# A two-layer MoE kernel after attention: the order of operand work and of weight loads in its second layer

## The chip, the cores and the metric

The kernel runs on one core of a Trainium2 chip. The metric is device time in microseconds (us). Three runs of the kernel before gave 1780.78, 1784.19 and 1786.06 us; the median is 1784.19 us. All numbers of a stretch or an instruction come from one further, profiled execution, which took 1785.07 us with a span of 1783.1 us.

## The reference

Attention with pooled keys and values gives 4608 tokens x 512. Two dense layers follow, each 512 -> 2048 -> 512. The second one, which the change touches, is:

```python
h = x @ w_in                      # (4608, 512) @ (512, 2048)
neg = h <= -1.0
pos = h >= 1.0
g = np.where(pos, h, np.where(neg, 0.0, (h + 1.0) ** 2 / 4.0))
return g @ w_out                  # (4608, 2048) @ (2048, 512)
```

## The kernel before

Every float32 operand of a matmul is split in two: a rounded part "hi" (written by ScalarE) and the rest "lo" = source - hi (written by VectorE). One product of blocks is then three matmuls: hi*hi, hi*lo, lo*hi.

The first layer runs token block by token block (lines 598 to 630) up to about 1002 us of the span. The second layer, class `Second`, uses block products: its matrices are cut in 2 x 2 blocks, and seven products of sums of blocks (a Strassen-Winograd form) replace eight. `ORDER1` = (1, 7, 2, 4, 6, 5, 3) is the order of the seven operands in its first phase (x @ w_in), `ORDER2` = (4, 5, 7, 6, 1, 3, 2) that of the second phase (g @ w_out).

**First phase.** Tokens go in six pairs of 2 x 384 columns, and for each pair there are eight steps j, so 48 steps, called cycles. A cycle has seven slots, in each of which TensorE does one product of six matmuls (128 x 128 by 128 x 384, line 841). The slots of a cycle hold products 6, 1, 7, 5, 2, 4, 3; products 1, 7, 2 and 4 already belong to the next step. So product 1 of a new pair is done in slot 1 of the last cycle of the pair before, product 4 in slot 5, and product 6 in slot 0 of the new pair's first cycle. X, V and Y are the PSUM banks in which products meet, p ("p7") and q are copies of banks in SBUF.

What else is issued stands in two places. `after(cycle, slot)` holds the same work for each cycle: three ScalarE copies, the four-step activation of the four results X, V, W, Y (`act1` on ScalarE, `act2` on VectorE or, for V and W, on GpSimd, `act3` on ScalarE, `act4` on VectorE), two VectorE adds, and the store of each result t to the DRAM buffer g. On VectorE these are 8 instructions a cycle. Two of them gate TensorE closely: the add of "W" (line 860, p<-Y,p) in slot 3 must have read bank Y before product 3 in slot 6 adds to it. The table in `first_phase` holds, per pair, the preparation of the next pair's operands: `x_load` (four DMAs of 384 KB, tiles xr), `x_sum` (the four block sums, two instructions each), and `x_split` (operand number pos of `ORDER1`, half k: one ScalarE and one VectorE instruction into a tile xs). An entry (c, s) is issued behind slot s of cycle c, counted from the start of the pair; the table runs from (4, 3) to (8, 0). The sums are made in place, so their order is tied to the splits: x_sum 2 overwrites the block b12 and can only follow its split. `w2_load`, `w2_sums`, `w2_split` prepare the weights of the second phase in the first four pairs and store them to DRAM (tiles w2d).

**Second phase.** Tokens go in blocks r of 1024; for each, seven products in `ORDER2` with eight units f each, a unit being 12 matmuls of 128 x 128 by 128 x 256 (line 1086). `g_load` brings g back (256 KB a load), `g_sum` makes sums, `hi` (line 1046) and `lo` (line 1051) split. The weights are fetched from w2d by `w2_fetch(t)`, 28 DMAs of 512 KB, four to a product, all of them issued during and just behind the last pair of the first phase.

**What sets the order.** The program is written in a fixed order; each engine runs its own instructions in that order and waits at the first that isn't ready. All DMAs are issued by one queue (SyncE). Its n-th DMA also waits until the DMA eight places before it has landed. A tile comes from a pool with a few places; a new tile in a place waits until the old one's last use, for a result t until its store has landed. The results t rotate over seven places ("gh" 2, "gl" 2, "raw" 3): each place is used again after seven results. The last places of "gh" serve unit 5 of the second phase as its hi and lo tiles.

Of the kernel before, what the change touches and what calls it, by code (L numbers as in the profile page):

```python
# [8 lines left out]
F32 = mybir.dt.float32  # L9
# [8 lines left out]
P = 128  # L18
NB = 512
# [8 lines left out]
NH = 384  # L28
# [7 lines left out]
def attention_moe_moe2(ctx: ExitStack, tc: tile.TileContext, qT, kT, v, k01, v01, w_in1, w_out1, w_in2, w_out2, out):  # L36
# [5 lines left out]
    nc = tc.nc  # L42
# [15 lines left out]
    raw_p = ctx.enter_context(tc.tile_pool(name="raw", bufs=3))  # L58
# [614 lines left out]
    class Second:  # L673
# [6 lines left out]
        def __init__(self, free):  # L680

            self.p1 = ctx.enter_context(tc.tile_pool(name="p1", bufs=1))
            used = sorted(
                [(2 * f + (1 if kind == "i" else 2 * LAG), kind, f) for kind in "io" for f in range(NF)]
            )
            tags = [f"{kind}{f}" for _, kind, f in used]
            self.spare, self.tags = tags[:4], tags[4:]
            order = [free] + [i for i in range(3) if i != free]
            self.x_tags = [[f"x{i}{k}{w}" for k in range(2) for w in "hl"] for i in order]
            self.wtmp = self.p1.tile([P, 6, 256], F32, tag="s7", name="wtmp")  # L690
            self.w1, self.w1_tiles, self.xs, self.bank, self.kept = {}, {}, {}, {}, {}
            self.g = [dram.tile([P, NT], F32, name=f"g2_{f}") for f in range(NF)]
            self.w2d = {pos: dram.tile([P, self.NJ, 2, 256], F32, name=f"w2d{pos}") for pos in range(7)}
            self.n_t = 0
            self.plan, self.places = {}, {}
            self.a, self.s, self.n_u = {}, {}, 0
            self.units = [(r, pos, f) for r in range(self.NPAIR2) for pos in range(7) for f in range(self.NJ)]
# [53 lines left out]
        def x_sum(self, what):  # L751

            for k in range(2):
                (b11, b12), (b21, b22) = self.kept["x", k, 0], self.kept["x", k, 1]
                to, a, b = {
                    1: (b11, b12, b11), 3: (b12, b22, b12), 2: (b12, b22, b11), 4: (b21, b21, b12),
                }[what]
                engine = nc.vector if what == 2 else nc.gpsimd
                engine.tensor_tensor(out=to, in0=a, in1=b, op=ALU.subtract)

        def x_split(self, p, pos, k):
            (b11, b12), (b21, b22) = self.kept["x", k, 0], self.kept["x", k, 1]
            prod = ORDER1[pos]
            if k == 0:
                self.xs[p, prod] = self.x_slot(7 * p + pos)
            src = {1: b11, 7: b12, 2: b21, 4: b21, 6: b12, 5: b11, 3: b22}[prod]
            s = self.xs[p, prod]
            self.parts(s[k, 0], s[k, 1], src, nc.gpsimd if k and prod in (5, 3) else nc.vector)

        def w2_load(self, f):  # L770
            t = wpool.tile([P, 2, DM], F32, tag=self.spare[0], name=f"w2x{f}")
# [25 lines left out]
        def ahead(self, slot):  # L797
            for j in range(self.NJ - 1):
                begin = (7 * j + 1) // 2 + 8
                if slot == begin - 6:  # L800
                    self.w1_load(j)
                if slot == begin - 2:
                    self.w1_sums(j)
                for pos in range(7):
                    if slot == begin + (pos + j % 2) // 2:
                        self.w1_split(j, pos)
            if slot == 5:
                self.x_load(0)
            for at, f, *args in (
                (9, self.x_split, 0, 0, 0), (10, self.x_split, 0, 0, 1), (11, self.x_sum, 1), (12, self.x_sum, 3),  # L810
                (14, self.x_split, 0, 1, 0), (15, self.x_split, 0, 1, 1), (16, self.x_sum, 2),
                (17, self.x_split, 0, 2, 0), (18, self.x_split, 0, 2, 1), (20, self.x_sum, 4),
                (22, self.x_split, 0, 5, 0), (23, self.x_split, 0, 5, 1),
                (24, self.x_split, 0, 6, 0), (25, self.x_split, 0, 6, 1),
            ):
                if slot == at:
                    f(*args)
# [43 lines left out]

        def t_tile(self, name):
            self.n_t += 1
            pool, tag = ((g_p, "gh"), (raw_p, "raw"), (g_p, "gl"), (g_p, "gh"), (raw_p, "raw"), (g_p, "gl"), (raw_p, "raw"))[
                self.n_t % 7
            ]
            return pool.tile([P, NB], F32, tag=tag, name=name)[:, 0:NH]


# [30 lines left out]
        def first_phase(self):  # L900
            for pos, k in ((3, 0), (3, 1), (4, 0), (4, 1)):
                self.put(-1, 0, self.x_split, 0, pos, k)
            self.put(-1, 1, self.w1_split, self.NJ - 2, 6)
            for pos in range(7):
                self.put(0, pos, self.w1_split, self.NJ - 1, pos)
            self.w1_load(self.NJ - 1)
            self.put(-1, 2, self.w1_sums, self.NJ - 1)
            for p in range(1, self.NPAIR):
                c = self.NJ * (p - 1)
                for cycle, slot, f, *args in (  # L910
                    (4, 3, self.x_load, p),
                    (5, 5, self.x_split, p, 0, 0), (5, 6, self.x_split, p, 0, 1),
                    (6, 0, self.x_sum, 1), (6, 1, self.x_sum, 3),
                    (6, 3, self.x_split, p, 1, 0), (6, 4, self.x_split, p, 1, 1), (6, 5, self.x_sum, 2),
                    (6, 5, self.x_split, p, 2, 0), (6, 6, self.x_split, p, 2, 1), (6, 6, self.x_sum, 4),
                    (7, 0, self.x_split, p, 4, 0), (7, 1, self.x_split, p, 4, 1),
                    (7, 2, self.x_split, p, 3, 0), (7, 3, self.x_split, p, 3, 1),
                    (7, 4, self.x_split, p, 5, 0), (7, 5, self.x_split, p, 5, 1),
                    (7, 6, self.x_split, p, 6, 0), (8, 0, self.x_split, p, 6, 1),
                ):  # L920
                    self.put(c + cycle, slot, f, *args)
            for f in range(self.NJ):
                n = 7 * (self.NJ * (f // 2) + 2 * (f % 2)) + 2
                self.put(n // 7, n % 7, self.w2_load, f)
                self.put((n + 6) // 7, (n + 6) % 7, self.w2_sums, f)
                for pos in range(7):
                    self.put((n + 8 + pos) // 7, (n + 8 + pos) % 7, self.w2_split, f, pos)
            end = self.STEPS - 1
            for f in range(4):
                self.put(end - 1, 3, self.g_load, 0, (2, 2), f)  # L930
                self.put(end - 1, 4, self.g_load, 0, (2, 2), f + 4)
                self.put(end, 1, self.g_load, 0, (2, 1), f)
                self.put(end, 4, self.g_load, 0, (2, 1), f + 4)
            for u in range(3):
                self.put(end, 3 + u, self.hi, u)
                self.put(end, 4 + u, self.lo, u)
            for cycle in range(-1, self.STEPS):
                for slot, (prod, ahead) in enumerate(((6, 0), (1, 1), (7, 1), (5, 0), (2, 1), (4, 1), (3, 0))):
                    s = cycle + ahead
                    self.product(prod, s)  # L940
                    self.after(cycle, slot)
                    for f, args in self.plan.pop((cycle, slot), []):
                        f(*args)
                if cycle >= self.STEPS - self.NJ:
                    for t in range(28):
                        if (2 * t + 1) // 7 == cycle % self.NJ:
                            self.w2_fetch(t)
            for slot in range(6):
                self.after(self.STEPS, slot)

        def after(self, c, slot):
# [8 lines left out]
                self.add("V", "V", "q", c)  # L960
            elif slot == 2:
                self.copy("p7", "V", c + 1)
                self.act1("V", c)
                self.act2("V", c)
                self.act2("Y", c - 1)
                self.act4("X", c)
            elif slot == 3:
                self.add("W", "Y", "p7", c)
                self.act4("Y", c - 1)
            elif slot == 4:  # L970
                self.act1("W", c)
                self.act2("W", c)
            elif slot == 5:
                self.act1("X", c + 1)
                self.act3("V", c)
            else:
                self.act4("V", c)
# [88 lines left out]
        def second_phase(self):  # L1066
# [7 lines left out]
            for u, (r, pos, f) in enumerate(self.units):  # L1074
                prod = ORDER2[pos]
# [15 lines left out]
                self.lo(u + 4)  # L1091
                if u + 7 < NU:
                    self.g_sum(*self.units[u + 7])
                if prod == 7:
                    self.g_load(r, (1, 2), f)
                elif prod == 1:
# [324 lines left out]
```

## Time and profile before

| | us |
|---|---|
| median of three runs | 1784.19 |
| profiled execution | 1785.07 |
| its span | 1783.1 |
| attention and first layer, to | 1002 |
| second layer, first phase | 1002 to 1392 |
| second layer, second phase | 1392 to 1783 |

The page gives TensorE (PE) as busy for 1690.8 us, 95% of the span, VectorE (DVE) for 72%, ScalarE (ACT) for 48%, GpSimd (POOL) for 37%. The shares are means over stages; what a stage loses is read from its own stretch, from the time between the starts of matmuls and from the clock that TensorE was granted, which the page shows in tenths (9 stands for 90% or more).

### The profile page before, as it was taken

How to read it: one execution, taken by the hardware profiler on the slowest of the kernel's cores; microseconds unless marked ns; L12 is line 12 of the kernel's file. 1: busy time of each engine (PE TensorE's matmuls, PEld its weight loads, DVE VectorE, ACT ScalarE, POOL GpSimd, SP SyncE). 2: the span in 40 equal slices, each digit the busy share in tenths (PEclk: the TensorE clock that was granted, in tenths of full speed). 3: DMA queues.
4: the chain of work that ended last, by engine and by line, in shares of the span. 5: the costliest groups of instructions: out<-in, count | busy, mean ns of one | idle time of the engine just before them, and what ended most of it. 6: DMA issues, size and time to landing. Idle time of an engine off the chain costs nothing.

```text
span 1783.1 us, 27980 instructions
## 1 busy us (share of the span) xinstructions
PE 1690.8 (95%) x9372; PEld 1493.2 (84%) x9372; DVE 1278.1 (72%) x2426; ACT 863.2 (48%) x1873; POOL 664.2 (37%) x762
## 2 busy tenths in 40 slices
PE   6688999999999999999999999999999599999999
PEld 4466778778888888888888889999999599999998
DVE  7987875666666566675547776786775488888967
ACT  4544443443444343443335566776666344444445
POOL 4764421222222122222214454554443335242535
PEclk9889999999999999999999999999999799999999
DMA  6423332213232322322131265456339833444331
GB/s 208 144 74 101 117 119 94 91 54 114 73 97 89 95 69 74 108 67 78 42 107 60 92 216 202 162 208 229 111 127 311 311 108 130 119 148 137 119 108 60
DMA packets 154224, 221.52 MB, mean 124 GB/s; under 512 B 18592, under 2 KB 95392, under 8 KB 154080
## 3 DMA queue, kind: packets, MB, share of 16 engines
q1 hardware_dynamic: 154080, 219.73, 37.6%
q8 instruction: 74, 1.21, 0.3%
q14 instruction: 70, 0.57, 0.1%
HBM read 136.84 MB, written 82.84 MB: 123 GB/s over the span
## 4 chain that ended last, share of the span: by engine, by line
PE 69%; DVE 16%; DMA 7%; issue 3%; ACT 2%; SPq 1%; POOL 1%; DVEq 0%; ACTq 0%; POOLq 0%
PE u L1086 20%; PE acc L628 6%; PE acc L629 6%; PE acc L630 6%; PE h L598 6%; PE h L599 6%; PE h L600 6%; PE Y L841 5%; PE V L841 3%; PE X L841 2%; PE sc L422 2%; DMA g<-tW 1%; DVE xs L705 1%; PE tm L478 1%; DMA w2d<-w2o 1%
## 5 line engine op out<-in xcount | busy, mean ns | idle before, releaser
L1086 PE MATMUL u<-v,m 128*128 128x256 f32 x3024 | 368.4, 285 | 18.6 <-DVE m L1051 12.2
L1086 PEld LDWEIGHTS u<-v,m 128*128 128x128 f32 x3024 | 366.3, 193 | 20.9 <-DVE m L1051 13.5
L1051 DVE TENSOR_TENSOR m<-m,m 128x512 fp32r<-128x512 f32 (+1 forms) x280 | 248.3, 917 | 70.5 <-ACT m L1046 49.6
L1046 ACT ACTIVATE m<-m 128x512 fp32r<-128x512 f32 (+1 forms) x280 | 162.8, 588 | 204.4 <-PE u L1086 136.4
L628 PE MATMUL acc<-gh,w0o 128*128 128x512 f32 x576 | 234.1, 406 | 9.8 <-ACT gh L133 9.5
L599 PE MATMUL h<-xl,w0i 128*128 128x512 f32 x576 | 226.5, 393 | 6.7 <-DVE xl L184 5.9
L629 PE MATMUL acc<-gl,w0o 128*128 128x512 f32 x576 | 229.2, 398 | 2.5 <-DVE gl L135 2.5
L598 PE MATMUL h<-xh,w0i 128*128 128x512 f32 x576 | 230.5, 400 | 0.8 <-DMA xh<-xk 0.8
L630 PE MATMUL acc<-gh,w0o 128*128 128x512 f32 x576 | 227.5, 395 | 0.0
L600 PE MATMUL h<-xh,w0i 128*128 128x512 f32 x576 | 225.8, 392 | 0.0
L612 DVE TENSOR_TENSOR h<-h,t 128x512 f32<-128x512 f32 x136 | 94.4, 694 | 138.3 <-ACT t L610 138.2
L610 ACT ACTIVATE t<-h 128x512 f32<-128x512 f32 x144 | 85.9, 597 | 165.6 <-PE h L600 98.7
L133 ACT ACTIVATE gh<-h 128x512 fp32r<-128x512 f32 x136 | 81.4, 599 | 131.2 <-DVE h L612 130.7
L455 POOL TENSOR_TENSOR at<-at,r 128x32 f32<-128x32 f32 (+3 forms) x160 | 68.9, 451 | 194.6 <-DVE r L452 192.4
L628 PEld LDWEIGHTS acc<-gh,w0o 128*128 128x128 f32 x576 | 109.6, 190 | 37.6 <-ACT gh L133 13.0
L599 PEld LDWEIGHTS h<-xl,w0i 128*128 128x128 f32 x576 | 109.2, 190 | 30.1 <-DVE xl L184 7.0
L629 PEld LDWEIGHTS acc<-gl,w0o 128*128 128x128 f32 x576 | 109.6, 190 | 27.5 <-DVE gl L135 6.7
L598 PEld LDWEIGHTS h<-xh,w0i 128*128 128x128 f32 x576 | 109.2, 190 | 24.5 <-DMA xh<-xk 1.7
L630 PEld LDWEIGHTS acc<-gh,w0o 128*128 128x128 f32 x576 | 109.7, 190 | 23.3
L600 PEld LDWEIGHTS h<-xh,w0i 128*128 128x128 f32 x576 | 109.0, 189 | 22.9
L135 DVE TENSOR_TENSOR gl<-h,gh 128x512 fp32r<-128x512 f32 x136 | 93.3, 686 | 47.6 <-ACT gh L133 46.6
L884 POOL TENSOR_SCALAR tV<-tV 128x384 f32<-128x384 f32 x48 | 56.3, 1173 | 132.4 <-ACT tV L876 130.8
(272 smaller groups left out, 3326.0 us busy)
## 6 DMA issues: line engine op xcount, KB each, us to landing
m<-g SPq DMA_DIRECT2D x128, 256.0 KB
w2d<-w2o SPq DMA_DIRECT2D x56, 256.0 KB
v<-w2d SPq DMA_DIRECT2D x28, 512.0 KB
x<-o SPq DMA_DIRECT2D x36, 256.0 KB
xr<-x SPq DMA_DIRECT2D x24, 384.0 KB
g<-tX SPq DMA_DIRECT2D x48, 192.0 KB
g<-tV SPq DMA_DIRECT2D x48, 192.0 KB
g<-tW SPq DMA_DIRECT2D x48, 192.0 KB
```

Source lines behind the costliest of these rows:

```text
L135: engine.tensor_tensor(out=lo, in0=src, in1=hi, op=ALU.subtract)
L598: nc.tensor.matmul(ph, wh[:, c], xh, start=k == 0, stop=False)
L599: nc.tensor.matmul(ph, wh[:, c], xl, start=False, stop=False)
L600: nc.tensor.matmul(ph, wl[:, c], xh, start=False, stop=k == KT - 1)
L612: nc.vector.tensor_tensor(out=g, in0=ph, in1=t, op=ALU.max)
L628: nc.tensor.matmul(acc, wh[:, c], gh, start=st, stop=False)
L629: nc.tensor.matmul(acc, wh[:, c], gl, start=False, stop=False)
L630: nc.tensor.matmul(acc, wl[:, c], gh, start=False, stop=sp)
L841: nc.tensor.matmul(ps, w[:, c], x[k, i], start=begin and k == n == 0, stop=k == 1 and n == 2, skip_group_check=True,)
L1046: nc.scalar.activation(out=self.s[u][0], in_=self.unit_source(u), func=AF.Copy)
L1051: nc.vector.tensor_tensor(out=lo, in0=self.unit_source(u), in1=hi, op=ALU.subtract)
L1086: nc.tensor.matmul(ps, a[:, c], w, start=begin and i == 0, stop=f == self.NJ - 1 and i == 2, skip_group_check=True,)
```

## The change

The change has four parts.

1. *Sums and operands of a new pair.* `x_sum` 2 goes to GpSimd and writes a tile of its own (x2s: half k = 0 in a place of "raw", half k = 1 in a tile "e") instead of overwriting b12. `x_sum` 4 goes from GpSimd to VectorE. The lo parts of the last two operands' second halves go from GpSimd to VectorE. The table is new: the splits start at (5, 2) instead of (5, 5), end at (8, 2) instead of (8, 0), and operand 3 of `ORDER1` (product 4) comes before operand 4 (product 6). `x_load` moves by one slot, the `w2` work by one slot as well.
2. *Results t* rotate by three pools (gh, raw, gl) in turn: a place of "gh" or "gl" is used again after six results, one of "raw" after nine.
3. *`act1` and `act2` of V* are issued behind slot 3 instead of slot 2.
4. *`w2_fetch`*: eight of the 28 fetches stay in the last pair; the other 20 are issued in the second phase, four in each of its first five products, for the product after next.

```diff
         def x_sum(self, what):
             for k in range(2):
                 (b11, b12), (b21, b22) = self.kept["x", k, 0], self.kept["x", k, 1]
...
+                if what == 2:
+                    pool, tag = ((raw_p, "raw"), (self.p1, "e"))[k]
+                    self.n_x2 += 1
+                    self.kept["x2", k] = pool.tile([P, NB], F32, tag=tag, name=f"x2s{self.n_x2}")[:, 0:NH]
+                t2 = self.kept.get(("x2", k))
+                to, a, b = {1: (b11, b12, b11), 3: (b12, b22, b12), 2: (t2, b22, b11), 4: (b21, b21, t2)}[what]
+                engine = nc.vector if what == 4 else nc.gpsimd
...
-            src = {1: b11, 7: b12, 2: b21, 4: b21, 6: b12, 5: b11, 3: b22}[prod]
+            src = {1: b11, 7: b12, 2: b21, 4: b21, 6: self.kept.get(("x2", k)), 5: b11, 3: b22}[prod]
...
-            self.parts(s[k, 0], s[k, 1], src, nc.gpsimd if k and prod in (5, 3) else nc.vector)
+            self.parts(s[k, 0], s[k, 1], src)
...
-            pool, tag = ((g_p, "gh"), (raw_p, "raw"), (g_p, "gl"), (g_p, "gh"), (raw_p, "raw"), (g_p, "gl"), (raw_p, "raw"))[
-                self.n_t % 7
-            ]
+            pool, tag = ((g_p, "gh"), (raw_p, "raw"), (g_p, "gl"))[self.n_t % 3]
...
-                    (4, 3, self.x_load, p),
-                    (5, 5, self.x_split, p, 0, 0), (5, 6, self.x_split, p, 0, 1),
...
+                    (4, 4, self.x_load, p),
+                    (5, 2, self.x_split, p, 0, 0), (5, 3, self.x_split, p, 0, 1),
...
-                n = 7 * (self.NJ * (f // 2) + 2 * (f % 2)) + 2
+                n = 7 * (self.NJ * (f // 2) + 2 * (f % 2)) + 3
...
-                        if (2 * t + 1) // 7 == cycle % self.NJ:
+                        if t < 8 and (2 * t + 1) // 7 == cycle % self.NJ:
                             self.w2_fetch(t)
...
             elif slot == 2:
                 self.copy("p7", "V", c + 1)
-                self.act1("V", c)
-                self.act2("V", c)
...
             elif slot == 3:
+                self.act1("V", c)
+                self.act2("V", c)
...
+                if r == 0 and pos < 5 and f < 4:
+                    self.w2_fetch(4 * (pos + 2) + f)
```

VectorE, before, in the cycle in which pair 1 takes over from pair 0: xs11, xs10 and xs12 are operand tiles of the new pair, xs10 that of product 4 (its halves x00 and x01; l is lo) and xs11 that of product 6; p77 is the add of "W" in slot 3, q7 that of "V" in slot 1; tW, tX, tY are results.

```order
L895 TENSOR_TENSOR tW6_10211<-p76_10102,tW6_10211 128x384
L860 TENSOR_TENSOR q7_10248<-V7_10178,q7_10248 128x384
L705 TENSOR_TENSOR xs11_x11l_10255<-xr1_10_10041,xs11_x11h_10254 128x384
L882 SCALAR_TENSOR_TENSOR tY6_10267<-tY6_10267 128x384
L895 TENSOR_TENSOR tX7_10222<-X7_10162,tX7_10222 128x384
L705 TENSOR_TENSOR xs10_x00l_10290<-xr1_01_10039,xs10_x00h_10289 128x384
L860 TENSOR_TENSOR p77_10185<-Y7_10169,p77_10185 128x384
L895 TENSOR_TENSOR tY6_10267<-Y6_10088,tY6_10267 128x384
L705 TENSOR_TENSOR xs10_x01l_10292<-xr1_11_10043,xs10_x01h_10291 128x384
```

The same place of VectorE in the change, with the same names:

```order
L705 TENSOR_TENSOR xs10_x00l_10257<-xr1_01_10050,xs10_x00h_10256 128x384
L895 TENSOR_TENSOR tW6_10219<-p76_10104,tW6_10219 128x384
L863 TENSOR_TENSOR q7_10252<-V7_10184,q7_10252 128x384
L705 TENSOR_TENSOR xs10_x01l_10259<-xr1_11_10054,xs10_x01h_10258 128x384
L883 SCALAR_TENSOR_TENSOR tY6_10271<-tY6_10271 128x384
L896 TENSOR_TENSOR tX7_10233<-X7_10166,tX7_10233 128x384
L863 TENSOR_TENSOR p77_10191<-Y7_10173,p77_10191 128x384
L896 TENSOR_TENSOR tY6_10271<-Y6_10090,tY6_10271 128x384
L705 TENSOR_TENSOR xs11_x10l_10303<-x2s3_10180,xs11_x10h_10302 128x384
L705 TENSOR_TENSOR xs11_x11l_10305<-x2s4_10182,xs11_x11h_10304 128x384
```

The operand of product 4 now stands before p77 instead of around it, and that of product 6 behind it. Counted from tW5, the first VectorE instruction behind slot 1 of the pair's cycle 6, the last lo of product 4 was the 24th VectorE instruction and is the 18th; p77 was the 22nd and is the 21st; the last lo of product 6 was the 18th and is the 24th.

SyncE, before, where the first phase ends: m are loads of g for the second phase, v2_24 to v2_27 the last weight fetches, tV47, tW47 and tY47 the last results on their way to g.

```order
L1017 DMA m15_13771<-g2_7_8749 128x512
L898 DMA g2_15_8757<-tV47_13747 128x384
L984 DMA v2_24_13788<-w2d6_8764 128x1024
L984 DMA v2_25_13790<-w2d6_8764 128x1024
L984 DMA v2_26_13792<-w2d6_8764 128x1024
L984 DMA v2_27_13794<-w2d6_8764 128x1024
L898 DMA g2_15_8757<-tW47_13764 128x384
L898 DMA g2_7_8749<-tY47_13797 128x384
L1017 DMA m15_13771<-g2_0_8742 128x512
```

The same place of SyncE in the change:

```order
L1018 DMA m15_13751<-g2_7_8749 128x512
L899 DMA g2_15_8757<-tV47_13736 128x384
L899 DMA g2_15_8757<-tW47_13744 128x384
L899 DMA g2_7_8749<-tY47_13769 128x384
L1018 DMA m15_13751<-g2_0_8742 128x512
L1018 DMA m15_13751<-g2_1_8743 128x512
L1018 DMA m18_13778<-g2_2_8744 128x512
L1018 DMA m18_13778<-g2_3_8745 128x512
L1018 DMA m18_13778<-g2_4_8746 128x512
L1018 DMA m27_13782<-g2_5_8747 128x512
L1018 DMA m28_13784<-g2_6_8748 128x512
L1018 DMA m29_13786<-g2_7_8749 128x512
```

The fetches are gone from between the last results and the loads of g; the first of the 20 stands behind m29.

## Rows read from the trace of the kernel before

**Rows 1.** Windows: stretch, length, busy us (count) per engine, clock, DMA share, GB/s.
```profile
1002.15:1392.35 390.20, 370.78 (x2018) 361.22 (x2016) 276.86 (x520) 257.87 (x569) 188.12 (x171) 0.96 0.57 198
1392.35:1432.20 39.85, 21.88 (x148) 20.56 (x147) 21.24 (x22) 11.06 (x21) 17.12 (x11) 0.77 0.71 259
```
**Rows 2.** Chain of waits: start, us, what; undisturbed matmuls of both phases.
```profile
1142.60 1.04 PE V L841 x6
1432.17 326.74 PE u L1086 x2716
```
**Rows 3.** Waits of PE, 1002 to 1385: who, for whom, us, times, longest.
```profile
PE V L841 <- ACT xs L704: 8.8, 4, 2.2
PE Y L841 <- DVE p L860: 2.0, 5, 0.6
```
**Rows 4.** Timeline of PE at the first and the last takeover: start, us, what.
```profile
1064.71 1.21 PE L841 MATMUL X<-xs,v 128*128 128x384 f32 x6
1068.12 0.44 PE L841 MATMUL V<-xs_x00h,v 128*128 128x384 f32 x1 [2.20 <-ACT xs_x00h L704]
1078.81 1.20 PE L841 MATMUL X<-xs,v 128*128 128x384 f32 x6
...
1325.19 1.21 PE L841 MATMUL X<-xs,v 128*128 128x384 f32 x6
...
1338.80 1.20 PE L841 MATMUL X<-xs,v 128*128 128x384 f32 x6
```
**Rows 5.** Windows, as Rows 1, behind the first takeover's wait.
```profile
1069.60:1076.40 6.80, 6.19 (x20) 6.08 (x20) 3.55 (x7) 3.64 (x9) 2.22 (x2) 0.50 0.20 70
```
**Rows 6.** Timelines of DVE, ACT and POOL before the first takeover's wait.
```profile
1055.59 1.37 DVE L895 TENSOR_TENSOR tW<-p,tW 128x384 f32<-128x384 f32 x1
...
1062.00 0.54 DVE L705 TENSOR_TENSOR xs<-xr,xs 128x384 fp32r<-128x384 f32 x1
...
1068.80 0.54 DVE L860 TENSOR_TENSOR p<-Y,p 128x384 f32<-128x384 f32 x1
...
1067.04 0.61 ACT L876 ACTIVATE tV<-q,half 128x384 f32<-128x384 f32 x1 [2.21 <-DVE q L860]
...
1055.28 1.26 POOL L759 TENSOR_TENSOR xr<-xr 128x384 f32<-128x384 f32 x1 [0.50 <-DVE xs L705]
```
**Rows 7.** Timeline of PE where the second phase starts.
```profile
1390.31 2.16 PE L841 MATMUL Y<-xs,v 128*128 128x384 f32 x6 [1.56 <-DVE p L860]
...
1407.02 0.79 PE L1086 MATMUL u<-v,m 128*128 128x256 f32 x2 [6.37 <-ACT m L1046]
1416.83 9.37 PE L1086 MATMUL u<-v,m 128*128 128x256 f32 x60 [9.01 <-DVE m L1051]
```
**Rows 8.** Timelines of ACT and DVE at the same place.
```profile
1406.34 1.67 ACT L1046 ACTIVATE m<-m 128x512 fp32r<-128x512 f32 x3 [10.16 <-DMA g<-tY]
...
1416.08 0.69 DVE L1051 TENSOR_TENSOR m<-m,m 128x512 fp32r<-128x512 f32 x1 [18.24 <-DMA g<-tY]
```
**Rows 9.** Timeline of SP's DMA issues at the same place.
```profile
1384.86 6.52 SPq L1017 DMA_DIRECT2D m<-g  x8
...
1399.58 0.32 SPq L898 DMA_DIRECT2D g<-tY  x1
...
1405.21 1.97 SPq L984 DMA_DIRECT2D v<-w2d  x4
...
1408.31 0.40 SPq L898 DMA_DIRECT2D g<-tY  x1
```
**Rows 10.** Behind the load of pair 1: an SP issue, ACT's timeline, a DMA of the chain.
```profile
1047.58 0.42 SPq L898 DMA_DIRECT2D g<-tV  x1
...
1051.47 0.56 ACT L876 ACTIVATE tX<-X,half 128x384 f32<-128x384 f32 x1
...
1054.57 0.49 ACT L854 ACTIVATE q<-Y 128x384 f32<-128x384 f32 x1 [1.30 <-PE Y L841]
...
1048.75 4.59 DMA g<-tW
```

More of the change, by code (lines that the diff above doesn't have):

```diff
@@ L693, in __init__ @@
             self.w2d = {pos: dram.tile([P, self.NJ, 2, 256], F32, name=f"w2d{pos}") for pos in range(7)}
-            self.n_t = 0
+            self.n_t = self.n_x2 = 0
             self.plan, self.places = {}, {}
@@ L754, in x_sum @@
                 (b11, b12), (b21, b22) = self.kept["x", k, 0], self.kept["x", k, 1]
[L755 to L758, printed above, removed]
+                if what == 2:
[5 more added lines that the diff above has]
+                engine = nc.vector if what == 4 else nc.gpsimd
                 engine.tensor_tensor(out=to, in0=a, in1=b, op=ALU.subtract)
@@ L810, in ahead @@
                 (9, self.x_split, 0, 0, 0), (10, self.x_split, 0, 0, 1), (11, self.x_sum, 1), (12, self.x_sum, 3),
-                (14, self.x_split, 0, 1, 0), (15, self.x_split, 0, 1, 1), (16, self.x_sum, 2),
+                (13, self.x_sum, 2), (14, self.x_split, 0, 1, 0), (15, self.x_split, 0, 1, 1),
                 (17, self.x_split, 0, 2, 0), (18, self.x_split, 0, 2, 1), (20, self.x_sum, 4),
@@ L910, in first_phase @@
                 for cycle, slot, f, *args in (
-                    (4, 3, self.x_load, p),
-                    (5, 5, self.x_split, p, 0, 0), (5, 6, self.x_split, p, 0, 1),
[L913 to L919, printed above, removed]
+                    (4, 4, self.x_load, p),
+                    (5, 2, self.x_split, p, 0, 0), (5, 3, self.x_split, p, 0, 1),
+                    (5, 4, self.x_sum, 1), (5, 6, self.x_sum, 3), (6, 1, self.x_sum, 2),
+                    (6, 2, self.x_split, p, 2, 0), (6, 3, self.x_split, p, 2, 1), (6, 4, self.x_sum, 4),
+                    (6, 4, self.x_split, p, 1, 0), (6, 6, self.x_split, p, 1, 1),
+                    (7, 0, self.x_split, p, 3, 0), (7, 1, self.x_split, p, 3, 1),
+                    (7, 3, self.x_split, p, 4, 0), (7, 4, self.x_split, p, 4, 1),
+                    (7, 6, self.x_split, p, 5, 0), (8, 0, self.x_split, p, 5, 1),
+                    (8, 1, self.x_split, p, 6, 0), (8, 2, self.x_split, p, 6, 1),
                 ):
```

## The prediction

> **What bounds the kernel now.** I read the windows of the second layer first, then the chain for the time of an undisturbed matmul, then TensorE's waits and its timeline, and last the timelines of whoever it waits for.
>
> The first phase holds 2016 matmuls in 390.20 us [rows 1]. Six undisturbed ones take 1.04 us [rows 2], so 336 products need 349.4 us: 40.8 us are lost. The second phase loses at its start: 148 matmuls in 39.85 us at a granted clock of 0.77 [rows 1], where a matmul undisturbed takes 326.74 / 2716 = 0.120 us [rows 2], so 17.8 us of work and 22.0 us lost. Elsewhere TensorE is full.
>
> Of the 40.8 us the waits name a cause: product 4 waits for the hi part of its operand in four places and, under another tile name, in a fifth, 2.2 us each; the next entry is 2.0 us over five waits for line 860 [rows 3]. That is once per takeover of a new pair, five times. The timeline shows what one costs: from product 2 at 1064.71 to the next product 2 at 1078.81 are seven products, 14.10 us instead of 7.28, so 6.82 us; at the last one 13.61, so 6.33 [rows 4]. The three between, read in the same way, lose 5.56, 6.12 and 6.08. Together 30.9 us. About half is waiting; behind the wait the clock stands at 0.50 for 6.8 us [rows 5], 1.2 instead of 2.4 GHz, which costs 3.4 us.
>
> The wait is VectorE's. From 1055.59 to 1068.80 it is full but for 0.17 us: 21 instructions in 13.21 us [rows 6]. The add q<-V,q comes so late that ScalarE stands 2.21 us in front of it, and the operand's hi part is queued behind. VectorE is slow there because an instruction with both inputs in SBUF takes 1.37 us while GpSimd makes a sum, and 0.54 us otherwise [rows 6].
>
> At the start of the second phase unit 5 waits 6.37 us for its hi and then 9.01 us for its lo part [rows 7]. Neither is short of work: the tiles lie in places whose results have not landed; ScalarE waits 10.16 us and VectorE 18.24 us for a store g<-tY [rows 8]. These stores leave late, at 1399.58 and 1408.31, since SyncE's queue, eight DMAs deep, holds 512 KB weight fetches and 256 KB loads ahead of them [rows 9].
>
> **The change, part by part.**
>
> *Takeover of a pair.* Per pair VectorE gets two lo parts more, loses the two of sum 2 and gets the two of sum 4; GpSimd's sums and lo parts go from eight to six. What counts is the run from tW5. The add p77, which product 3 of the last cycle needs, was its 22nd instruction and is its 21st; product 4's last lo was the 24th and is the 18th. Back to back two starts lie about 0.47 us apart, by the same run: 13.21 us less five stretches by GpSimd of together 3.2 us and the gap of 0.17 are 9.84 us for 21 steps. In the change only sum 2 falls beside this run, on two instructions of which each may be stretched by 0.83 us (1.37 - 0.54); with what is left of sum 3, I take 2.0 us. Then product 4's operand is ready 17 x 0.47 + 2.0 + 0.54 = 10.5 us behind 1055.59, at 1066.1. Product 4 would start at 1065.75 and needs its last lo with its fifth matmul, at 1066.45: no wait. p77 ends at 1055.59 + 20 x 0.47 + 2.0 + 0.54 = 1067.5; product 3 would start at 1066.79: late by 0.7. The add of the cycle before moves from 5th to 6th place, behind an extra lo part: 1055.59 + 5 x 0.47 + 1.7 + 0.54 = 1060.2, for a product at 1059.51: late by 0.7, which then covers part of the other. Product 6 needs the 24th at about 1068.5 and gets it at 1068.9. So the long wait goes and two or three short ones at line 860 come: I take 1.5 us per takeover (between 0, if GpSimd's sums fall on instructions that read PSUM, which show no stretch, and the present 3.2 us of idle time). Whether the clock still falls then no row settles; five waits of up to 0.6 us [rows 3] left it at full. I take one fall in three: 5 x 3.4 / 3 = 5.7 us. Saved: 30.9 - 7.5 - 5.7 = 17.7 us; the bounds are 0 and 30.9.
>
> *Results in turn over three pools.* This adds a wait. A place of gh or gl comes back after six results: the new X in slot 5 takes the place of V from one cycle before, stored six products earlier, 6.2 us. In most cycles the store has long landed. Behind `x_load` it has not: V's store is issued at 1047.58 behind 1.5 MB, the W store after it needs 4.59 us from 1048.75, and the X that would take V's place is at 1051.47 [rows 10]. So ScalarE waits up to 1.9 us there, where the rotation puts the two in one pool (four of the five pairs). Queued behind it are act3 of V and the copy q; ScalarE is idle for 1.30 us before that copy anyway [rows 10], so about 0.6 us is passed on, which the 1.5 us above holds. From below it is nothing, if V's store lands before the last load.
>
> *act1 of V one slot later.* ScalarE no longer stands in front of the add in slot 1 but does the copies first. No time of its own; its cover is that act3 comes two slots later.
>
> *x_load, w2 work one slot later.* The order among themselves stays, and SyncE's next entry was waiting for a result in either place. Taken as 0, bounds +-2 us (the five waits of rows 3 lie there).
>
> *Weight fetches.* Twenty of 28 leave the queue before the second phase: seven of them stood between the loads of g at 1384.86 and the store at 1408.31 [rows 9]. At the 259 GB/s of that stretch [rows 1] their 3.7 MB are 14.2 us. What is left ahead of the last store tY is 16 loads of 256 KB and seven results of 192 KB, 5.6 MB: 21.6 us from 1384.2 on at that rate, less while the queue is full. I take 1403 for its landing instead of 1416.08. TensorE has five units, 1392.35 + 60 x 0.12 + 0.8 = 1400: unit 5 waits about 3 us instead of 15.4. The catching up behind it (VectorE makes lo parts and sums beside GpSimd) costs 5 us now and I leave it. 22.0 becomes 8.4: saved 13.6 us, between 8 (the 8-deep queue holds the store back as before but for the fetches' half) and 20. The first phase's last wait, 1.56 us [rows 7], hangs on the tail's own chain; 0.5 saved.
>
> The fetches return in the second phase: 10.5 MB in five products of 11.6 us. Behind the loads of the first block nothing in SyncE's queue waits for TensorE, so the first nine run ahead, some 20 us before use. The rest stand behind loads that wait for VectorE to free a place, some 20 units ahead. At 259 GB/s four fetches and eight loads, 4.2 MB, take 16 us against 11.6 in the two products in which both run: 9 us of a lead of 20. Cost 0, and 9 us if that lead weren't there.
>
> **Sum.** 17.7 + 13.6 + 0.5 = 31.8 us. 1785.07 - 31.8 = 1753.3 for the profiled execution, which is 0.9 above the median: 1752.
>
> **The rivals.**
>
> *B, the takeover only moves its wait.* VectorE's work up to p77 falls by one instruction of 22. If GpSimd's sums stretch more than I take, TensorE waits at product 3 instead of product 4 and the clock falls as before. For it: VectorE has no slack in that run. Against: product 4's operand is 6 places earlier. Only the start gains: 1784.2 - 14 = 1770. The Trainium skill (Perfetto Trace Analysis, Optimizing Scalar/DVE Operations) says that VectorE and GpSimd share an SBUF read port, so that moving work between the two might not help. By that rule sum 2 costs VectorE on GpSimd what it cost there, and only the two GpSimd instructions that go count, less the two that come: 2 x (0.83 - 0.47) = 0.7 us per takeover, which gives B 3.5 us more, 1767. The stretch to 1.37 us agrees with it; the instructions that read PSUM show none beside the same sums.
>
> *C, all of both losses goes.* 30.9 + 20 + 1: 1732. For it: sums start earlier, when VectorE still waits for ScalarE. Against: the store tY.
>
> *D, slower: the shorter rotation.* In four pairs ScalarE waits for V's store behind x_load. From 1.30 us on it holds up the copy q, and VectorE, full afterwards, can't make it up. If it waits for 4.6 us, a whole store behind the loads, 3.3 us pass on with a further fall of the clock, 3.4 us, in each of four pairs: 26.8 us, and the takeover's own loss stays. With 13.6 won at the start: 1797. For it: rows 10. Against: the store is issued 3.9 us before X comes.
>
> **How the numbers follow.** Chances: forecast 0.60, with its own range 1742 to 1762; B 0.22; C 0.12; D 0.06. The range that should hold 8 in 10 takes in B and stops short of C's end: 1736 to 1771. Within 0.3%, 5.4 us, a measurement can't tell a change from none. Faster: the forecast, C and nearly all of B, 0.92; no change 0.03, from B's upper side; slower 0.05 from D.
>
> **What would show it.** Right: no wait of product 4 for a hi part at takeovers, short waits for line 860 in place of it; granted clock at full in most takeovers; no fetch of weights among SyncE's last loads before the second phase; ScalarE's wait for g<-tY there under 5 us; waits of ScalarE's tX for a store g<-tV behind x_load. Wrong: waits over 1.5 us and half clock at all takeovers (B), ScalarE's tX waiting more than 3 us (D), or TensorE waiting for weight tiles v in the second phase.

## The result, and the profile after

The changed kernel takes 1766.58 us (median of four runs, 1765.43 to 1769.35) against 1784.62 us before: 0.9905 of the time, 95% interval 0.9885 to 0.9924. It is faster by 18.0 us; 31.8 were forecast. The time lies in the range of 1736 to 1771, but outside the forecast's own 1742 to 1762, and just below rival B (1767 to 1770). The kernel also prepares pair 0 in the new order, at the end of the first layer (`ahead`: `x_sum` 2 in slot 13 instead of 16, and on GpSimd), which "The change" does not list.

The two phases' windows of the profiled execution (span 1764.9 us), as in [rows 1]:

```profile
1004.16:1387.10 382.94, 362.79 (x2018) 352.26 (x2016) 278.11 (x532) 261.42 (x573) 177.44 (x162) 0.99 0.54 186
1387.10:1421.50 34.40, 28.04 (x209) 27.23 (x209) 28.43 (x29) 12.14 (x22) 20.03 (x12) 0.93 0.82 304
```

Less its 349.4 us of products the first phase loses 33.5 us (40.8 before). In the second window 209 matmuls of 0.12 us leave 9.3 us lost (22.0 before). So the start gained 12.7 us of its 13.6; the first phase gained 7.3 of 18.2.

TensorE's longest waits in the first phase, without the one at its very end, to compare with [rows 3] (who, for whom, us, times, longest):

```profile
PE Y L844 <- DVE p L863: 16.2, 19, 2.6
PE X L844 <- ACT Y L857: 0.7, 1, 0.7
PE Y L844 <- ACT q L857: 0.6, 1, 0.6
```

Product 4's long waits for hi parts are gone. In their place product 3 waits for the add p, 19 times instead of five. TensorE's timeline, [rows 4], at the first and the last takeover:

```profile
1061.26 0.34 PE L844 MATMUL V<-xs_x11h,v 128*128 128x384 f32 x1
1064.20 2.29 PE L844 MATMUL Y<-xs,v 128*128 128x384 f32 x6 [2.61 <-DVE p L863]
...
1319.47 0.44 PE L844 MATMUL Y<-xs_x00h,v 128*128 128x384 f32 x1 [0.65 <-DVE p L863]
```

At the five takeovers this wait is 2.61, 2.20, 1.13, 2.56 and 0.65 us. From the starts of matmuls, less 0.1734 us each, the takeovers (cycle 5 of a pair to cycle 0 of the next) lose 5.2, 4.1, 4.0, 5.1 and 1.9 us: 20.3 together, 30.9 before, 13.2 forecast. The first four overlap with preparation of w2 in the same pair, the fifth does not.

The windows behind the first, second, fourth and fifth of these waits, as [rows 5]; the clock stands behind the five engines:

```profile
1064.20:1068.00 3.80, 3.80 (x13) 3.80 (x14) 3.80 (x8) 2.41 (x5) 2.71 (x3) 0.56 0.16 58
1129.80:1137.00 7.20, 7.20 (x41) 7.05 (x42) 7.20 (x15) 6.43 (x14) 3.44 (x4) 1.00 0.25 87
1257.50:1262.50 5.00, 4.45 (x17) 4.46 (x18) 4.88 (x10) 3.13 (x7) 3.26 (x3) 0.66 0.26 93
1319.40:1326.00 6.60, 6.53 (x37) 6.40 (x38) 6.60 (x14) 6.17 (x14) 2.84 (x4) 1.00 0.26 91
```

The clock fell at two takeovers of five, the first and the fourth, for 3.4 us each; at half clock that costs 1.7 us each. The other 16.9 of the 20.3 us are lost at full clock.

VectorE at the first takeover, as [rows 6], from tV to the add p that product 3 waits for:

```profile
1057.43 1.12 DVE L896 TENSOR_TENSOR tV<-q,tV 128x384 f32<-128x384 f32 x1 [1.44 <-ACT tV L890]
1058.47 1.37 DVE L883 SCALAR_TENSOR_TENSOR tX<-tX 128x384 f32<-128x384 f32 x1
1059.76 1.37 DVE L896 TENSOR_TENSOR tW<-p,tW 128x384 f32<-128x384 f32 x1
1061.05 0.55 DVE L863 TENSOR_TENSOR q<-V,q 128x384 f32<-128x384 f32 x1
1061.52 0.89 DVE L883 SCALAR_TENSOR_TENSOR tY<-tY 128x384 f32<-128x384 f32 x1
1062.33 0.55 DVE L896 TENSOR_TENSOR tX<-X,tX 128x384 f32<-128x384 f32 x1
1062.80 0.88 DVE L705 TENSOR_TENSOR xs<-xr,xs 128x384 fp32r<-128x384 f32 x1
1063.60 0.55 DVE L863 TENSOR_TENSOR p<-Y,p 128x384 f32<-128x384 f32 x1
```

and three of the same instructions at the fifth takeover:

```profile
1312.60 1.19 DVE L896 TENSOR_TENSOR tV<-q,tV 128x384 f32<-128x384 f32 x1 [1.24 <-ACT tV L890]
...
1315.00 1.37 DVE L896 TENSOR_TENSOR tW<-p,tW 128x384 f32<-128x384 f32 x1
...
1318.87 0.54 DVE L863 TENSOR_TENSOR p<-Y,p 128x384 f32<-128x384 f32 x1
```

From tW to p the run takes 3.84 us in one and 3.87 in the other. The difference is where it begins. Product 3 was due at 1061.26 + 0.17 = 1061.43, 1.67 us behind tW; at the fifth, at 1319.47 less its 0.81 of delay, 1318.66, 3.66 us behind tW. ScalarE and GpSimd show why. First takeover:

```profile
1052.37 0.53 ACT L704 ACTIVATE xs<-xr 128x384 fp32r<-128x384 f32 x1 [0.77 <-DMA xr<-x]
1054.87 0.53 ACT L704 ACTIVATE xs<-xr 128x384 fp32r<-128x384 f32 x1 [1.47 <-DMA xr<-x]
1055.30 0.60 ACT L877 ACTIVATE tW<-p,half 128x384 f32<-128x384 f32 x1
...
1055.98 1.17 POOL L885 TENSOR_SCALAR tW<-tW 128x384 f32<-128x384 f32 x1 [1.33 <-DVE xs L705]
1057.12 2.31 POOL L762 TENSOR_TENSOR xr<-xr 128x384 f32<-128x384 f32 x2
```

Fifth:

```profile
1309.90 0.53 ACT L704 ACTIVATE xs_x11h<-xr 128x384 fp32r<-128x384 f32 x1
...
1312.35 2.30 POOL L762 TENSOR_TENSOR xr<-xr 128x384 f32<-128x384 f32 x2
```

The first splits wait for the x loads; behind them in ScalarE's queue stands tW, behind tW's min on GpSimd the sums. The sums begin 3.7 us after the last add p (1053.41) at the first takeover and 2.5 us after it (1309.88) at the fifth. ScalarE's last step of tV is queued behind these splits too, and VectorE's tV, at the head of the run, waits for it: it starts 4.00 us ahead of product 3's time at the first takeover (1057.43) and 6.06 us ahead at the fifth (1312.60).

Why the loads come late stands in SyncE's queue. Its issues at the first takeover, then at the fifth, and its waits before these loads in the whole phase:

```profile
1047.46 0.38 SPq L797 DMA_DIRECT2D w2d<-w2o  x1
1047.94 2.51 SPq L739 DMA_DIRECT2D xr<-x  x4
...
1303.94 1.81 SPq L739 DMA_DIRECT2D xr<-x  x4
...
SPq L739 <- DMA w2d<-w2o: 3.0, 4, 0.8
```

Cycle 5 of the pair begins at 1047.79 and at 1305.14. So the loads leave 0.15 us behind its start at the first takeover (0.15 to 0.17 at the first four) and 1.20 us ahead of it at the fifth. At the first four the last stores of w2o stand ahead of them, and SyncE waits in the loads until such a store has landed, four times. In the kernel before it has no wait there, the loads leave 0.30 us ahead of cycle 5, and the first split comes three slots later.

The second phase's start: TensorE, [rows 7]; then who unit 5 waits for, [rows 8]; then SyncE's issues, [rows 9].

```profile
1385.01 2.29 PE L844 MATMUL Y<-xs,v 128*128 128x384 f32 x6 [1.56 <-DVE p L863]
1387.10 8.17 PE L1087 MATMUL u<-v,m 128*128 128x256 f32 x62
1398.60 8.95 PE L1087 MATMUL u<-v,m 128*128 128x256 f32 x60 [3.33 <-DVE m L1052]
...
1392.76 1.68 ACT L1047 ACTIVATE m<-m 128x512 fp32r<-128x512 f32 x3 [2.50 <-DMA g<-tY]
...
1397.85 0.69 DVE L1052 TENSOR_TENSOR m<-m,m 128x512 fp32r<-128x512 f32 x1 [5.15 <-DMA g<-tY]
...
1392.28 0.36 SPq L899 DMA_DIRECT2D g<-tY  x1
1392.69 5.92 SPq L1018 DMA_DIRECT2D m<-g  x8
1398.65 6.94 SPq L985 DMA_DIRECT2D v<-w2d  x9
```

The last store leaves with no fetch among the loads ahead of it. And ScalarE's wait of tX, for which [rows 10] had stood:

```profile
ACT tX L877 <- DMA g<-tV: 0.5, 1, 0.5
```

### The profile page after: what moved, and what is told of

Same layout as the page of the kernel before. It is cut to its first block, busy times and chain, and to the rows that moved or that the text cites. A ratio compares the mean times of both kernels' runs of the same rounds, so it can differ in the third digit from the quotient of the medians.

```text
span 1764.9 us, 27969 instructions
## 1 busy us (share of the span) xinstructions
PE 1682.3 (95%) x9372; PEld 1485.6 (84%) x9372; DVE 1276.4 (72%) x2438; ACT 864.6 (49%) x1873; POOL 649.6 (37%) x750
## 4 chain that ended last, share of the span: by engine, by line
PE 72%; DVE 14%; DMA 6%; issue 4%; ACT 3%; POOL 1%; SPq 1%; ACTq 0%; DVEq 0%; POOLq 0%
PE u L1087 20%; PE Y L844 6%; PE acc L628 6%; PE acc L629 6%; PE acc L630 6%; PE h L598 6%; PE h L599 6%; PE h L600 6%; PE V L844 3%; PE X L844 3%; PE sc L422 2%; PE tm L478 1%; DMA m<-g 1%; DVE h L612 1%; DMA g<-tV 1%
```

## The experiments

All kernels ran beside the kernel before. "Lost" is the first phase less 349.4 us in the profiled execution, "takeovers" the five together, "else" the rest of it without the tail (2.7 to 5.7 us), "start" the first 60 us of the second phase. One profile is uncertain by some us: fetches alone leaves the takeovers as they were and shows 27.5 instead of 30.9, and single takeovers with equal code differ by up to some 2 us (experiment 3). The profile of 6 is of its longest execution, 1781.84 us, 6.4 above its median.

| | median us | ratio to before, 95% | lost | takeovers | else | start |
|---|---|---|---|---|---|---|
| before | 1784.62 | | 40.8 | 30.9 | 6.3 | 22.4 |
| the change | 1766.58 | 0.9885 to 0.9924 | 33.5 | 20.3 | 9.5 | 9.5 |
| 1 fetches alone | 1770.04 | 0.9903 to 0.9947 | 36.4 | 27.5 | 5.3 | 9.8 |
| 2 without them | 1781.89 | 0.9973 to 1.0003 | 38.2 | 21.9 | 10.6 | 19.4 |
| 3 loads early | 1763.34 | 0.9865 to 0.9906 | 31.5 | 20.1 | 8.6 | 9.6 |
| 4 sums early | 1759.91 | 0.9843 to 0.9892 | 26.2 | 14.2 | 8.3 | 8.7 |
| 5 seven in turn | 1764.73 | 0.9873 to 0.9903 | 30.7 | 19.6 | 8.3 | 10.9 |
| 6 V back | 1775.47 | 0.9936 to 0.9969 | 45.2 | 24.2 | 18.2 | 9.9 |
| 7 slot back | 1759.28 | 0.9841 to 0.9870 | 25.8 | 14.5 | 8.5 | 9.5 |
| 8 spread | 1758.80 | 0.9832 to 0.9864 | 25.0 | 8.4 | 13.8 | 10.4 |
| 9 three slots | 1761.03 | 0.9851 to 0.9887 | 27.1 | 11.1 | 13.2 | 9.4 |
| 10 two slots | 1756.87 | 0.9835 to 0.9872 | 24.2 | 10.9 | 10.5 | 9.1 |
| 11 V and slot back | 1757.84 | 0.9842 to 0.9876 | 21.9 | 13.4 | 5.8 | 9.7 |
| 12 joined | 1755.28 | 0.9819 to 0.9857 | 20.9 | 10.2 | 7.9 | 10.2 |

**1 and 2: which part earns what.** Part 4 of the change alone, on the kernel before; and the change with these lines taken back.

```diff
-                        if (2 * t + 1) // 7 == cycle % self.NJ:
+                        if t < 8 and (2 * t + 1) // 7 == cycle % self.NJ:
...
+                if r == 0 and pos < 5 and f < 4:
+                    self.w2_fetch(4 * (pos + 2) + f)
```

> The kernel before with the weight fetches alone (8 in the last pair, 20 in the second phase). If the two gains add up, the first phase loses 40.6 us as before, the start of the second phase some 9.4 instead of 22.3, and the time is 1784.6 - 13 = 1771.6 us. If the start's gain hangs on the other parts (an earlier end of the operand work, other places for the results), unit 5 still waits over 8 us and the time is above 1776.

> The changed kernel with all 28 weight fetches back in and behind the last pair. If the gains add up, the first phase loses 33.4 us as in the changed kernel, the start of the second phase 22 us, and the time is 1784.6 - 5.5 = 1779 us. If the fetches in the last pair cost the takeover part something, the first phase loses more in its last eight cycles, by some us, and the time is above 1781.

The gains add up within the uncertainty: 14.1 by the fetches and 2.2 by the rest (against 1784.13 in these runs), 18.0 together. The fetch part is as forecast. The operand part, forecast at 18.2, can't be told from no change by itself; its takeovers lose 21.9. Its time lies above the 1781 of the second case of its expectation, and as in that case the fetches cost the first phase's last eight cycles something: they lose 8.1 us instead of 4.7 in the change.

**3 and 4: late loads or the sums themselves.** Both move part of the weights' preparation and load x early for two pairs; 4 also moves the splits of the first operand and the sums 1, 3, 2 one cycle ahead for these pairs, such as:

```diff
-                n = 7 * (self.NJ * (f // 2) + 2 * (f % 2)) + 3
+                n = 7 * (0, 2, 8, 10, 16, 18, 24, 32)[f] + 3
-                    (4, 4, self.x_load, p),
+                    ((2, 5) if p > 3 else (4, 4)) + (self.x_load, p),
...
+                    ((4, 4) if p > 3 else (5, 4)) + (self.x_sum, 1),
```

> The changed kernel with the weights' preparation spread over five pairs (2, 2, 2, 1, 1 instead of 2, 2, 2, 2), which lets the x loads for the pairs 4 and 5 leave 13 slots earlier; splits and sums stay in their slots. Theory 'late loads': ScalarE's waits for xr (0.5 and 1.6 us at pair 4) start the sums 1.2 us late; without them takeover 4 loses about 2 us instead of 5.1, without a fall of the clock; takeover 5 stays at 1.9. Time 1763.5. Theory 'sums beside VectorE's run': takeover 4 still waits over 1.5 us for line 863, its loss stays above 4 us, time 1766.

> As the kernel with early loads, and for the pairs 4 and 5 also the first operand's splits and the sums 1, 3 and 2 one cycle earlier, so that none of GpSimd's sums lies beside VectorE's run in cycle 6. Theory 'sums beside VectorE's run': the waits for line 863 in these two takeovers fall under 0.5 us, both together lose under 1.5 us instead of 7.0, time 1761. Theory 'late loads' alone: the same as the kernel with early loads, within 1 us. A rival, 'VectorE has too many instructions there anyway': takeover 5 still waits 0.6 us or more.

With early loads takeover 4 loses 1.7 us instead of 5.1, with no wait for p in its cycle 6; takeover 5 1.6 instead of 1.9; the first three, unchanged in code, 5.2, 6.3 and 5.4. ScalarE's waits for xr at pair 4 are gone (the change had 0.5 and 1.6 us); from 1238 to 1255 us these two are all that it has:

```profile
ACT q L857 <- PE Y L844: 6.0, 3, 2.1
ACT tW L877 <- DVE p L863: 0.8, 2, 0.6
```

So late loads it is, by the profile; the times alone overlap, and the load can leave early only where the w2 work is thinned, so the run does not separate the two. With the sums early too, 4 and 5 lose 0.7 and 0.6, 1.0 us less each than with early loads alone: VectorE's run is unstretched then, tW to p 2.34 us instead of 3.84:

```profile
1248.48 0.56 DVE L896 TENSOR_TENSOR tW<-p,tW 128x384 f32<-128x384 f32 x1
...
1250.82 0.55 DVE L863 TENSOR_TENSOR p<-Y,p 128x384 f32<-128x384 f32 x1
```

**5 to 7: the parts that the prediction had costed at nothing.** 5 takes back the old turn of seven places; 6 moves `act1` and `act2` of V back behind slot 2; 7 moves the w2 work and `x_load` back by one slot. Their diffs in this order:

```diff
-            pool, tag = ((g_p, "gh"), (raw_p, "raw"), (g_p, "gl"))[self.n_t % 3]
+            pool, tag = ((g_p, "gh"), (raw_p, "raw"), (g_p, "gl"), (g_p, "gh"), (raw_p, "raw"), (g_p, "gl"), (raw_p, "raw"))[
+                self.n_t % 7
...
                 self.copy("p7", "V", c + 1)
+                self.act1("V", c)
+                self.act2("V", c)
...
             elif slot == 3:
-                self.act1("V", c)
-                self.act2("V", c)
...
-                n = 7 * (self.NJ * (f // 2) + 2 * (f % 2)) + 3
+                n = 7 * (self.NJ * (f // 2) + 2 * (f % 2)) + 2
-                    (4, 4, self.x_load, p),
+                    (4, 3, self.x_load, p),
```

> The changed kernel with the results t in the old turn of seven places. Outside the takeovers and the tail the first phase lost 6.2 us before and 9.4 in the change. Theory 'rotation': ScalarE's and VectorE's new waits for stores of t and of w2o (0.5 to 1.7 us each) make these 3.3 us; they fall back under 7 us and the takeovers by up to 1 us each, time 1762. Rivals 'act1 of V' and 'w2 work one slot later': the 9.4 us stay within 1 us, time 1766.

> The changed kernel with act1 and act2 of V back behind slot 2. Theory 'act1 of V': the copies and W's activation come earlier again against the add of slot 3 and the 9.4 us outside the takeovers fall under 7. Rivals 'rotation' and 'w2 work one slot later': 9.4 stays within 1 us. In either case ScalarE stands up to 2 us in front of q again, so that the waits in the takeovers may grow by 0.5 us each: time 1763 by the first, 1766 to 1769 by the rivals.

> The changed kernel with the w2 work and the x loads back in their slots of before (one slot, 1.04 us, earlier); splits and sums stay. Theory 'late loads': ScalarE waits some 1 us less for xr in each of the first four takeovers, which lose about 0.8 us less each: 20.3 becomes 17, time 1763. Theory 'w2 work one slot later' for the loss outside the takeovers: 9.4 falls under 7 as well, time 1760.5; its rivals 'rotation' and 'act1 of V': 9.4 stays.

The turn of the places is not told apart from nothing (intervals overlap). The slot is: 7.3 us by the medians, 7.7 of lost time, 5.8 of them in the takeovers, more than expected. The loads then leave 0.30 to 0.33 us ahead of cycle 5 at the first four takeovers, and SyncE no longer waits for a store of w2o before them. The clock falls at no takeover, which is 3.4 of the 5.8, and TensorE's waits for p, those at the very end included, are 12.8 us (17.7 in 20 waits in the change):

```profile
PE Y L844 <- DVE p L863: 12.8, 15, 1.7
```

"Else" stays at 8.5, so the w2 work's slot alone does not explain what is lost there. Six was a surprise, slower by 8.9. Outside the takeovers it loses twice as much, since GpSimd's queue now has V's min, which waits for ScalarE, ahead of the w2 sums:

```profile
1023.99 1.17 POOL L885 TENSOR_SCALAR tV<-tV 128x384 f32<-128x384 f32 x1 [4.13 <-ACT tV L877]
1025.12 0.74 POOL L784 TENSOR_TENSOR w2s<-w2x 128x256 f32<-128x256 f32 x1
```

ScalarE's splits of w2 then wait for these sums (eight waits in the whole first phase; 5.5 us in six in the change):

```profile
ACT w2o L704 <- POOL w2s L787: 23.4, 8, 2.9
```

Counted from the phase's start these sums stand 5.5 us later than in the change (17.9 us instead of 12.5). So V's slot can't be judged without the w2 slot. With the w2 work one slot late, V behind slot 2 puts its min ahead of the sums on GpSimd; with the w2 work in its place of before the sums stand first wherever V is.

**11: both back.** Experiments 6 and 7 in one.

> The changed kernel with the w2 work and the x loads one slot back and act1 and act2 of V back behind slot 2, both as before. With V alone moved back, GpSimd's w2 sums stood behind V's min and were 8.5 us late. Theory 'V costs only by that order': with the w2 work one slot back the sums stand ahead of it again, and the time is that with the slot back alone, 1759.3 within 2 us, the loss outside the takeovers 8.3 within 1. Rival 'V in slot 3 keeps ScalarE free for its copies and pays by itself': the takeovers lose over 18 us instead of 14.5, time 1763 or above.

(The 8.5 us in it are a difference of plain times; from the phase's start it is the 5.5 us above.)

"Else" falls to 5.8, as before the change (6.3), the takeovers to 13.4, and the clock stays full:

```profile
1007.25:1378.56 371.31, 358.67 (x2018) 348.17 (x2016) 275.51 (x531) 259.15 (x571) 179.32 (x162) 1.00 0.55 191
```

By time it is not told apart from 7, as the first theory said; against the change it is faster with intervals that don't meet. "Else" fell by 2.7, more than that theory allowed. V in slot 3 does not pay by itself.

**8 to 10: how far the loads can be moved.** 8 spreads the preparation as (0, 2, 8, 16, 24, 32, 40, 42), with early loads and sums for the pairs 2 to 5; 9 and 10 are kernel 4 with the w2 work at + 0 or + 1 instead of + 3 and the x loads of the pairs 1 to 3 at (4, 1) or (4, 2). Of 8 against 4 (where also `p > 1` stands for `p > 3`), and of 9 against 4:

```diff
-                n = 7 * (0, 2, 8, 10, 16, 18, 24, 32)[f] + 3
+                n = 7 * (0, 2, 8, 16, 24, 32, 40, 42)[f] + 3
-                        if t < 8 and (2 * t + 1) // 7 == cycle % self.NJ:
+                        if t < 8 and ((2 * t + 1) // 7 if t % 4 < 3 else 4) == cycle % self.NJ:
...
-                n = 7 * (0, 2, 8, 10, 16, 18, 24, 32)[f] + 3
+                n = 7 * (0, 2, 8, 10, 16, 18, 24, 32)[f] + 0
-                    ((2, 5) if p > 3 else (4, 4)) + (self.x_load, p),
+                    ((2, 5) if p > 3 else (4, 1)) + (self.x_load, p),
```

> The kernel with early sums, with the weights' preparation spread as 2, 1, 1, 1, 1, 2 over the six pairs, so that the x loads leave early and the sums stand a cycle earlier for the pairs 2 to 5 (fetches 3 and 7 of the eight wait for cycle 44). Theory 'late loads': four takeovers lose 0.7 us each, the first 4 to 5, together 8 instead of 20.3 in the change; time 1754. Rival 'the work of the last pair is in the way of the tail': the tail (3.7 us) or the start of the second phase (9.5 us) grows by 3 us or more, time 1758 or above.

> The kernel with early sums for the pairs 4 and 5, and for the pairs 1 to 3 the w2 work and the x loads three slots earlier than in the change (3.1 us). Theory 'late loads': ScalarE waits for no xr there, the takeovers 1 to 3 lose 1.6 us each instead of 4.0, 5.4 and 3.5, in all 6 with the last two; time 1759.9 - 8 = 1752. Rival 'w2 work in other places costs elsewhere': the loss outside the takeovers (8.1 us) grows by 3 or more, time 1755 or above.

> As the kernel with three slots, with two (2.1 us) instead. Theory 'late loads': the takeovers 1 to 3 lose some 2.2 us each, time 1754. Rival 'w2 work in other places costs elsewhere': the loss outside the takeovers differs from that with three slots by 2 us or more, and decides which of the two is the faster.

In 8 the four takeovers cost 0.6 to 0.7 us each, but the work in the last pair costs some 8 (cycles 42 to 44): ScalarE waits there for stores of w2o, 8.6 us in three waits, so the gain stays short of its forecast by 5 us, though not by the tail or the start. In 9 no split waits for xr any more and the takeovers 1 to 3 still lose 3.0, 2.8 and 4.1, so the loads are not all of it there; "else" grows by 4.9, and the time is above 1755, as the rival has it. ScalarE's waits for V's min are longer there (6.9 us in 4):

```profile
ACT tV L890 <- POOL tV L885: 10.4, 5, 2.6
```

10 lies between 4 and 9 in "else" (10.5), with takeovers 1 to 3 at 3.8, 2.6 and 3.4 instead of 2.2 each; its time is the lowest of these, but its interval overlaps with those of 7 and 9. What the takeovers 1 to 3 still lose in 9 no run settles.

**12: joined.** Kernel 4 with V and the w2 work back as in 11, x loads at (4, 3), and the loads that the first split needs first:

```diff
-            for k in range(2):
-                for r in range(2):
+            for r in range(2):
+                for k in range(2):
```

> Joined: the w2 work and act1 of V in their places of before, the x loads of the pairs 1 to 3 in slot (4, 3), the weights' preparation spread over five pairs with early loads and sums for the pairs 4 and 5, and the two x loads that the first split needs issued first. Theory 'late loads': takeovers 1 to 3 as with V and the slot back or less (2.9, 2.5, 3.7 us), 4 and 5 at 0.7 each; the loss outside the takeovers 5.6 as there; the first phase loses 18.7 us or less instead of 21.7 and the time is 1757.8 - 3 = 1755 us, with the loads' order up to 1 us less. Rival 'the V slot and the early sums get in each other's way', as the places of w2 and V did: takeovers 4 and 5 lose over 1.5 us each, time 1757 or above.

The time is as expected, the fastest median here, and faster than the change with intervals that don't meet. Against 11 the intervals overlap. Lost time was 20.9 instead of 18.7: takeovers 4 and 5 cost 0.5 each, but takeover 1 4.4 and "else" 7.9.

## Why the prediction was right, and where it was wrong

*Start of the second phase: right, in mechanism and size.* Saved 12.7 of 13.6 us. Unit 5 waits 3.33 us (3 forecast); the last tY store has landed 10.75 us into the phase (1397.85 less 1387.10) where 1403 meant 10.65 from 1392.35. The fetches in the second phase cost nothing that shows: TensorE waits for no v there, and the phase as a whole is 13.0 us shorter (377.8 instead of 390.8), its first 60 us 12.9. One sum was off: 22.0 less 15.4 plus 3 is 9.6, not the 8.4 that the prediction has; 9.3 were measured.

*Takeover: right mechanism, over-sized, by a step costed at nothing.* The run from tW to p was put at 5 x 0.47 + 1.7 = 4.05 us and is 3.84; at the fifth takeover tW stands 3.66 us ahead of product 3's time (3.92 in the plan) and TensorE waits 0.65 us (0.7 forecast). That takeover loses 1.9 us at full clock, where 1.5 had been taken. At the other four the run begins up to 2 us later, and all five lose 3.4 us each on average besides the clock. The step that failed is *x_load, w2 work one slot later*: "The order among themselves stays", it says, and takes it as 0 with bounds of +-2 us. The order does stay, but the first split was moved by three slots towards the loads in the same table, and the one slot took more of what was left. Measured: 7.3 us by time (experiment 7), more than three times the bound. The reason given looked at SyncE's entry behind the loads; in the change the loads themselves wait, four times, for stores of w2o, and one slot earlier they don't. No run moves the loads without the w2 work, so the shares of the two in the 7.3 us stay open. With it goes *act1 of V one slot later* ("No time of its own"): with the w2 work late V's slot is worth 8.9 us (experiment 6), with the w2 work in its place of before nothing that the times tell apart (7 against 11). With both taken back the first phase loses 21.9 us, where 40.8 - 17.7 - 0.5 = 22.6 had been forecast. In part that is luck: the takeovers lose 13.4 us there and 13.2 had been forecast, but as 7.5 us of waiting and 5.7 of falls of the clock, and in experiment 11 the clock doesn't fall.

*Elsewhere in the first phase* 3.2 us are lost anew (9.5 - 6.3), which the sum had not; with both slots back they are gone.

*The clock.* One fall in three was assumed, two of five occurred; they cost 3.4 us, 5.7 had been taken.

*The tail's 0.5 us* did not come: the wait for p there is 1.56 us as before. *The first layer* ended 2.0 us later; over the runs it ends between 1002.2 and 1007.3, with equal code at both 1002.7 and 1007.1. Of the 2.0 us 1.4 are there already 400 matmuls earlier (912.69 against 911.25 us), before pair 0 is loaded (922.16), so they aren't the change. These last 400 matmuls take 90.6 and 90.9 us in the two kernels with the old order for pair 0 and 91.3 to 92.3 in the twelve with the new one: a little of it, 0.4 us or more, may be that order. The profiled executions add up: 10.6 in the takeovers, 12.9 at the start, less 3.2 and 2.0, is 18.3; the spans differ by 18.2.

*The rivals.* B named the right place: the wait moved to product 3 and line 863, over 1.5 us at three takeovers of five. Its cause was not the main one: GpSimd's sums stretch VectorE no more than was taken (3.84 against 4.05), though without them takeovers 4 and 5 lose 1.0 us less each (experiments 3 and 4). That the clock falls at every takeover was wrong. That the time lies so near B's is in part chance: by time the operand part gains 2.2 to 3.9 us (18.0 less 14.1), little, as B has it, but by the profiles the takeovers gain 10.6, and the losses elsewhere hide part of it. The range holds the time because it takes in B's. D fell: ScalarE's tX waited 0.5 us once for the store of tV, and the old turn of places changes nothing that can be told. C fell with the waits for p.

## What to carry to other kernels

When a consumer is moved towards its load and the load moves too, the distance is a term of the sum: issue, landing, first use and what stands ahead of the load in its queue are read from the trace, not from the order in the table. A slot's shift that keeps the order of its own work can still change who stands first on another engine's queue. Undo "free" edits together as well as one by one: here one alone gained 7 us, the other alone lost 9, and only the pair brought the loss elsewhere back to what it had been.

## What the runs showed of the hardware

Beside GpSimd's work VectorE's stretch has no fixed size: tX and tW took 1.37 us, tY and the lo parts 0.88 to 0.89, the adds that read PSUM 0.55, as all do alone. What sets it is when GpSimd's instruction ends. GpSimd's sums at the first takeover, one by one:

```profile
1058.09 1.34 POOL L762 TENSOR_TENSOR xr<-xr 128x384 f32<-128x384 f32 x1
1059.38 1.33 POOL L762 TENSOR_TENSOR xr<-xr,xr 128x384 f32<-128x384 f32 x1
1060.67 1.32 POOL L762 TENSOR_TENSOR xr<-xr,xr 128x384 f32<-128x384 f32 x1
1061.95 1.31 POOL L762 TENSOR_TENSOR x2s<-xr,xr 128x384 f32<-128x384 f32 x1
```

They end at 1059.43, 1060.71, 1061.99 and 1063.26; tX, tW, tY and the lo part, which began at different distances, end at 1059.84, 1061.13, 1062.41 and 1063.68, each 0.41 or 0.42 us later. So do 28 of the 33 VectorE instructions over 0.7 us in the first phase that begin beside a sum of GpSimd.

Waits of similar size differ in what follows: behind 2.20 us the clock stayed at 1.00, behind 2.61 and 2.56 it was 0.56 and 0.66 (1.2 of 2.4 GHz for part of the stretch). Before the change it stood at 0.50 behind a wait of 2.20 us [rows 4, rows 5], with two shorter ones (0.36 and 0.61) close behind, and in the change behind the first phase's last wait, 1.56 us, as well (0.50 from 1385.1 to 1388.3). Why, no run here shows.
